# A gated mix of a long convolution and a token mixer on one core: first sine early, gate as array columns, four outputs finished in one step, two sets of transposes as transfers

## The chip, the cores and the metric

The kernel runs on one core of a Trainium2 chip. Its time is in device microseconds (us), from the start of the program to its end, as one launch. Five engines work side by side, each through its own list of instructions in order: TensorE (PE in the profile, with its weight loads as PEld), VectorE (DVE), ScalarE (ACT), GpSimd (POOL) and SyncE (SP), which here only issues transfers. An engine that waits for a semaphore holds up everything behind it in its own list.

## The reference

```python
def reference(A_q, A_k, A_v, A_shift_k, A_ssm_k, A_ssm_D, B_x, B_w1, B_w2, B_w3, B_w4, gate_w):
    x = A_q                                             # (1, 2048, 640), bf16
    g = sigmoid((x * gate_w).sum(-1, keepdims=True))
    # a: a causal convolution of 2048 taps for each of 640 channels, by FFT
    k_shift = sum over t < 4 of k_pad[:, t:t + S] * shift_k[:, 3 - t]
    kv = k_shift * v
    y = irfft(rfft(pad(kv)) * rfft(pad(ssm_k)))[:S] + kv * ssm_D
    a = x * y
    # b: layernorm, w1, gelu, a shift of the four channel quarters by +1, -1, +2, -2 tokens, w2
    h = gelu(layernorm(x) @ w1)                         # 640 -> 640
    x1 = x + shifted(h) @ w2                            # 640 -> 640
    b = x1 + gelu(layernorm(x1) @ w3) @ w4              # 640 -> 1536 -> 640
    return g * a + (1 - g) * b
```

## The kernel before

The 2048 tokens are held as 16 "slots" of 128 tokens (a token's partition comes from its high bits, its slot from the low four). The program is a list of some 770 small tasks. Each task names its engine, what it reads and writes, which buffers it takes and gives back. The order in which they are issued is written out by hand as a list of numbers (`ORDER`), the letter behind a number choosing the engine (a for ScalarE, v for VectorE, p for GpSimd). That one list fixes the order on each engine, and on SP that of the transfers. A small planner (`Plan.place`) walks through it only to choose buffers and the number of "fill" matmuls, which multiply zeros and keep TensorE's clock up where it expects a gap. PSUM has eight banks (pool `U`), taken singly or in pairs; transfers go out on eight semaphores in turn, so that the ninth one waits for the first to land.

The tasks that the change and the prediction name, with the lines of the profile:

| task | engine | what it does | line before |
|---|---|---|---|
| `fill` | PE | matmuls of zeros, 512 columns | 256 |
| `cjb.j`, `cj.j` | PE, ACT | row j of `shift_k` (transfer `ldCJ`) spread over all partitions, copied out of PSUM | 473, 387 |
| `phase`, `phsmall`, `phand`, `sin` | DVE, ACT | integer phases of the Fourier matrices from GpSimd's iotas, then one sine of 2272 columns into `TRIG` | 422 to 455, 459 |
| `st1.s`, `rs1.s`, `nm1.s` | DVE or ACT, POOL, DVE or ACT | mean and variance of slot s, its rstd, the normed rows | 521 to 542 |
| `tr1.s`, `ev1.s`, `evh.s` | PE, DVE or ACT | the normed rows of two slots transposed by TensorE, copied to `xnT`; halo slots | 548, 387/389 |
| `trh.c`, `evt.c` | PE, DVE or ACT | the filter `ssm_k` transposed | 762, 387/389 |
| `w1.G.p`, `g1`, `w2.s`, `x1.s`, `sq.s` | PE, ACT, PE, DVE, ACT | first MLP, gelu, second matrix, residual, sum of squares | 623/627, 640, 649, 656, 661 |
| `gate`, `gz`, `gtanh`, `gg` | PE, DVE, ACT, DVE | the gate's sums by token, and the two factors from them | 671/674, 681 to 684, 686, 691/692 |
| `kv3` ... `kv0` (`m`, `a`, `v`) | DVE | four taps, sums and the product with v, for four slots each | 782, 786, 790 |
| `s1h`, `s1x`, `e1h`, `e1x` | PE, ACT or DVE | first Fourier step of filter and of kv, copied to `FS` | 817/830, 387/389 |
| `wF`, `rF` | SP | `FS` written to DRAM, read back in another layout as `FX` | 842, 856 |
| `s2`, `e2`, `pa`/`pb`, `s3`, `e3` | PE, ACT/DVE, DVE, PE, ACT/DVE | second step, complex product, step back | 864, 387/389, 879, 892, 387/389 |
| `wG`, `rG`, `s4`, `yq` | SP, SP, PE, DVE | result through DRAM to `GX`, last step with matrix `BT`, times gate and q | 904, 924, 936, 942 |
| `bperm`, `trb`, `evb` | DVE, PE, DVE | the columns of `TRIG` put in order, 16 blocks transposed, copied to `BT` | 389, 917, 389 |
| `ve2`, `st2`, `nm2.s`, `dt2.s` | DVE, POOL, DVE or ACT, SP | second layernorm; a transfer that transposes a slot's normed rows | 700/701, 706 to 708, 540/542, 724 |
| `w3.c.f`, `g2.c.f`, `w4.s`, `t2.s` | PE, ACT, PE, DVE | third and fourth matrix for four slots (chunk c), residual | 732, 739, 746, 752 |
| `ad.s`, `st.s` | DVE, SP | the last mix, two slots stored together | 948, 382 |

The convolution and the MLP interleave. VectorE's `kv` work of the first half stands between the layernorms and the residuals; between the write of the last `wFx` and the first `s2` stand the four `w4` of chunk 0 on TensorE, and between the last `s3` and the first `s4` those of chunks 1 and 2.

Of the kernel before, what the change touches and what calls it, by code (L numbers as in the profile page):

```python
# [16 lines left out]
P = 128  # L17
# [19 lines left out]
0 60v 22 73a 1 74 7 2 21 20 23 71v 3 8 4 9 16 72 63a 5 64 61a 53v 70p 14 51v 62 12 54 79v 13a 75v 31 36 52 18 38  # L37
391 81v 6 66v 56v 24 17a 392v 32 82 89v 25 65a 15a 395 80 67 76v 30 34 90 396a 69v 387 388v 55v 77 37 83v 68a
393 47 35 57 78a 87a 84v 88 28 26 394v 389 97v 33 85 59a 86v 390v 92v 119 42 10 397 121 58a 98 27 95v 100v 113v
19 450 41 91a 93 94v 96 40 11a 99v 111v 39 400 120 451a 123 122 438 124 105v 439a 29 444 43 127 452 401 402 445a  # L40
440 441a 141 101 145 125 112 115v 398 128 102a 453a 142 146 44 149 150 442 446 106 126 443a 147 148 403 404 129
130 447a 454 405 143 114 138 139 455a 132 133 45 144 406 103a 154 155 456 458 399 157 116a 131 407 50 457a 104
107v 158 448 160 161 459a 411 449 108a 134 135 109 136 117 140 151 152 110a 118a 211 137 410 412 163 212 164 462
464 460 468 465a 463a 165 217 167 185 213v 469a 186 169 408 413 470 218 46 466 215v 409 168 221v 414 166 415 416
417 171 467a 471a 461 193 49 474 170 214 473 172 478 187 191 479a 176 177 421 472 194 475a 173 216 192 219a 480
174 220 188 420 482 189 481a 190 179 222 180 476 483a 477a 485 156 204 422 486 494 205 423 201 202 484 207 495a
490 492 424 48 208 487a 418 162 153 419 425 491a 488 489a 493a 223 496 198 224 498 199 497 500 501a 231 239 426
502 504 499a 506 232 243 503a 233 240 225 431 507a 182 427 430 432 505a 433 226 244 510 234 514 428 515a 509 183
# [12 lines left out]
691a 693 297 707 724 341 342 298 295 706 355 356 726 708 296 727 709 729 365 730 369 742 728 366 697 370 361 733
# [293 lines left out]
def build(env, nc, io):  # L355
# [36 lines left out]
    def c_iota(t):  # L392
# [3 lines left out]
        nc.gpsimd.iota(env.early("KC", [P, 64], I32)[:], pattern=[[4, 64]], base=1, channel_multiplier=0)  # L396
        nc.gpsimd.iota(env.early("PI", [P, 1], I32)[:], pattern=[[0, 1]], base=0, channel_multiplier=1)
# [3 lines left out]
    add("iota", "POOL", 2.2, c_iota, w=["iota"], roles=("C0",))  # L401

    def c_id(t):
        I = env["ID"]
        nc.gpsimd.memset(env["ONE"][:], 1.0)
        nc.gpsimd.memset(env.early("NPI", [P, 1], F32)[:], float(-np.pi * (1 - 2.0 ** -20)))
        nc.gpsimd.memset(I[:], 0.0)
        nc.gpsimd.affine_select(out=I[:], in_=I[:], compare_op=ALU.not_equal, fill=1.0, base=0, pattern=[[-1, P]],
                                channel_multiplier=1)
        nc.gpsimd.memset(env.sm("MH", [P, 2])[:], -0.5)  # L410
        nc.gpsimd.memset(env["K"][0:1, 0:3, :], 0.0)
    add("ident", "POOL", 2.9, c_id, w=["ID", "c0", ("K", "z")], roles=("C0", "K"))
# [27 lines left out]
    add("phsmall", "DVE", 2.6, c_small, r=["iota"], w=["ph0"], roles=("PRE", "C0"))  # L440
# [10 lines left out]
    for ri in range(2):  # L451
        add(f"phase{ri}", "DVE", 1.25, c_ph(ri), r=["iota"], w=[("ph", ri)], roles=("PRE", "C0"))
# [8 lines left out]
    add("sin", "ACT", 3.5, c_sin, r=["pha", "c0"], w=["TRIG"], roles=("PRE", "C0"))  # L461
# [94 lines left out]
    DMA1 = ()  # L556
# [108 lines left out]

    def gate(t):
        m = env.PS[:, t.buf["U"][0], :]
        gw = env.sm("GW", [P, 5], BF16)
        for s in range(16):
            for kb in range(5):  # L670
                nc.tensor.matmul(m[:, s:s + 1], lhsT=env["xnT"][:, s + 2, kb, :], rhs=gw[:, kb:kb + 1], start=(kb == 0),
                                 stop=(kb == 4))
        for kb in range(5):
            nc.tensor.matmul(m[:, 16:17], lhsT=env["ONE"][:], rhs=gw[:, kb:kb + 1], start=(kb == 0), stop=(kb == 4))
    tg = add("gate", "PE", 2.3, gate, r=["GW", "c0"] + [("xnT", s) for s in range(16)], acq=[ONE], mode="f", roles=("xnT",))

    def gz(t):
        m = env.PS[:, tg.buf["U"][0], :]
        z, sd = SS("Z"), SS("SD")
        sg = env.sm("SG", [P, 1])  # L680
        nc.vector.tensor_tensor(out=sd[:], in0=SS("VE")[:], in1=SS("RS")[:], op=ALU.mult)
        nc.vector.tensor_scalar(out=sg[:], in0=m[:, 16:17], scalar1=-1.0, scalar2=None, op0=ALU.mult)
        nc.vector.scalar_tensor_tensor(out=z[:], in0=SS("NB")[:], scalar=sg[:, 0:1], in1=m[:, 0:16], op0=ALU.mult, op1=ALU.add)
        nc.vector.tensor_tensor(out=z[:], in0=z[:], in1=sd[:], op=ALU.mult)
# [304 lines left out]
```

## Time and profile before

| | |
|---|---|
| time, median of 3 runs | 234.26 us (232.64 to 235.73) |
| the profiled execution | 233.85 us, of which 232.1 us are the span of its instructions |
| PE, DVE, ACT, POOL busy in the span | 95%, 81%, 67%, 17% |
| granted TensorE clock, mean | 0.988 |
| moved by transfers | 56.23 MB, 242 GB/s |

The span holds the core's instructions; 1.75 us of the execution lie outside it. A busy share is a mean over stages with different limits: what an edit is worth is read in its own stage, from the row of the wait that ends last there. In the chain of waits, each piece is what released the next, back from the last instruction. The busy time of a group of matmuls can be a little longer than the time that it takes from the chain, since matmuls overlap at their ends.

### The profile page before, as it was taken

Reading aid. Unit: us, or ns where it says so; the run is one execution under the profiler, and the core shown is the slowest. Engines: PE = TensorE matmul, PEld = TensorE weight load, DVE = VectorE, ACT = ScalarE, POOL = GpSimd, SP = SyncE. Lnnn points to the kernel's source line nnn. Section 1 sums busy time; section 2 is a strip of 40 time slices with the busy share of each in tenths; the row PEclk is TensorE's granted clock in tenths of the full one; section 3 lists DMA queues with packets and bytes.
Section 4 is the critical chain, followed back from the end, with each engine's and each line's share of the span. In section 5 each row is a group of like instructions: output and inputs, shape, how many; then the busy total and the mean of one; then the engine's idle time right before and its main releaser. Section 6 shows DMA issues by size and latency. Waiting matters only on the chain.

```text
span 232.1 us, 5340 instructions
## 1 busy us (share of the span) xinstructions
PE 220.8 (95%) x2143; PEld 108.6 (47%) x2163; DVE 186.9 (81%) x264; ACT 155.1 (67%) x221; POOL 40.5 (17%) x90
## 2 busy tenths in 40 slices
PE   7799999999999999999999999999999999999990
PEld 3158834456345744445543433344345554444550
DVE  5974699989999989997378998897986128887972
ACT  2996989988897998979669988888956004142000
POOL 7585317810700000011340000000000000000000
PEclk9979999999999999999999999999999999999998
DMA  5899889976999696867899995899843894968742
GB/s 149 280 277 303 198 237 272 330 270 206 289 294 283 196 266 224 270 224 250 191 315 300 327 349 177 255 228 310 204 172 135 242 406 147 282 187 248 233 109 57
DMA packets 39051, 56.23 MB, mean 242 GB/s; under 512 B 13809, under 2 KB 28914, under 8 KB 39026
## 3 DMA queue, kind: packets, MB, share of 16 engines
q1 hardware_dynamic: 39026, 55.88, 81.8%
q8 instruction: 17, 0.28, 0.5%
q14 instruction: 8, 0.07, 0.1%
HBM read 34.90 MB, written 18.35 MB: 229 GB/s over the span
## 4 chain that ended last, share of the span: by engine, by line
PE 80%; DVE 7%; DMA 4%; issue 2%; SPq 2%; ACT 2%; DVEq 0%; ACTq 0%
PE PS L746 21%; PE PS L732 18%; PE PS L649 8%; PE PS L623 7%; PE PS L864 4%; PE PS L892 4%; PE PS L762 3%; DMA FX<-FH 3%; PE PS L817 3%; DVE VC L786 3%; PE PS L256 2%; PE PS L936 2%; SPq L382 2%; PE PS L627 2%; DVE VC L782 2%
## 5 line engine op out<-in xcount | busy, mean ns | idle before, releaser
L746 PE MATMUL PS<-W,h2T 128*128 128x128 bf16 (+1 forms) x374 | 53.2, 297 | 0.5
L739 ACT ACTIVATE h2T<-PS 128x512 bf16<-128x512 f32 x48 | 28.1, 609 | 30.8 <-PE PS L732 30.0
L746 PEld LDWEIGHTS <-h2T 128*128 128x128 bf16 x384 | 29.6, 98 | 25.3 <-issue 2.5
L387 ACT CAST FS<-PS 128x1024 bf16<-128x1024 f32 x38 | 37.1, 1022 | 4.5 <-PE PS L817 2.6
L732 PEld LDWEIGHTS <-W 128*128 128x128 bf16 x240 | 21.2, 98 | 30.0 <-issue 8.5
L387 ACT CAST XH<-PS 128x1024 bf16<-128x1024 f32 x26 | 25.8, 1014 | 6.5 <-PE PS L864 6.4
L732 PE MATMUL PS<-x1nT,W 128*128 128x512 bf16 x120 | 28.8, 380 | 0.0
L732 PE MATMUL PS<-XB,W 128*128 128x512 bf16 x120 | 28.6, 380 | 0.0
L752 DVE TENSOR_TENSOR x<-PS,x 128x640 bf16<-128x640 f32 x16 | 13.1, 822 | 15.8 <-PE PS L746 15.8
L879 DVE TENSOR_TENSOR PP<-XH 128x2048 bf16<-128x2048 bf16 x20 | 23.6, 1219 | 0.9 <-PE PS L892 0.4
L782 DVE TENSOR_TENSOR VC<-K,VC 128x2560 bf16<-128x2560 bf16 x16 | 23.8, 1485 | 0.2
L649 PE MATMUL PS<-W,hsT 128*128 128x128 bf16 (+1 forms) x152 | 23.1, 295 | 0.4
L623 PE MATMUL PS<-xnT,W 128*128 128x512 bf16 x80 | 19.1, 380 | 0.5 <-ACT hsT L640 0.5
L389 DVE CAST XH<-PS 128x1024 bf16<-128x1024 f32 x14 | 16.7, 1219 | 2.8 <-PE PS L864 2.7
L649 PEld LDWEIGHTS <-hsT 128*128 128x128 bf16 x160 | 12.9, 98 | 11.5 <-issue 0.2
L786 DVE TENSOR_TENSOR VC<-VC 128x2560 bf16<-128x2560 bf16 x12 | 17.9, 1489 | 0.2
L942 DVE SCALAR_TENSOR_TENSOR W<-PS,GG,QO 128x640 bf16<-128x640 f32 x16 | 13.6, 879 | 4.4 <-PE PS L936 3.9
L706 POOL TENSOR_TENSOR r<-v,MH 128x2 f32<-128x2 f32 x8 | 6.9, 856 | 55.6 <-DVE v L701 55.5
L387 ACT CAST GS<-PS 128x1024 bf16<-128x1024 f32 x13 | 13.0, 1018 | 3.1 <-PE PS L892 3.1
L656 DVE SCALAR_TENSOR_TENSOR x<-PS,x 128x640 bf16<-128x640 f32 x16 | 13.1, 820 | 2.3 <-PE PS L649 2.0
L948 DVE SCALAR_TENSOR_TENSOR QO<-x,OG,W 128x640 bf16<-128x640 bf16 x16 | 13.6, 879 | 0.1
L864 PE MATMUL PS<-FX,TRIG 64*32 64x512 bf16 x320 | 12.9, 382 | 0.1
(106 smaller groups left out, 272.4 us busy)
## 6 DMA issues: line engine op xcount, KB each, us to landing
FH<-FS SPq DMA_DIRECT2D x8, 640.0 KB, 5.4
FXD<-FS SPq DMA_DIRECT2D x8, 640.0 KB, 4.6
FX<-FXD SPq DMA_DIRECT2D x10, 512.0 KB, 5.5
FX<-FH SPq DMA_DIRECT2D x10, 512.0 KB, 5.2
GX<-GD SPq DMA_DIRECT2D x8, 640.0 KB, 5.2
W<-in_B_w_dram SPq DMA_DIRECT2D x2, 1920.0 KB, 10.5
GD<-GS SPq DMA_DIRECT2D x8, 480.0 KB, 3.8
x<-in_A_q_dram SPq DMA_DIRECT2D x16, 160.0 KB, 4.9
```

Of the source, the lines that this page charges most:

```text
L387: nc.scalar.copy(out=out, in_=in_)
L389: (nc.vector if t.on == "DVE" else nc.gpsimd).tensor_copy(out=out, in_=in_)
L623: nc.tensor.matmul(m[:, b, :], lhsT=W[:, 0, kb, 160 * fb:160 * fb + 128], rhs=rhs(kb, shifts[fb]), start=(kb == 0), stop=(kb == 4))
L649: nc.tensor.matmul(m[:, c0:c1], lhsT=env["hsT"][:, o.buf["hs"][0], fb, 128 * (s % 4):128 * (s % 4) + 128], rhs=env["W12"][:, 1, fb, c0:c1] ...
L732: nc.tensor.matmul(env.PS[:, t.buf["U"][0], :], lhsT=env["W3"][:, kb, 128 * fb:128 * fb + 128], rhs=env.nT(int(nP[-1]))[:, :, kb, :], star ...
L739: nc.scalar.activation(out=env["h2T"][:, o.buf["h2"][0], fb, :], in_=env.PS[:, t.buf["U"][0], :], func=ACT.Gelu_apprx_tanh)
L746: nc.tensor.matmul(m[:, c0:c1], lhsT=env["h2T"][:, o.buf["h2"][0], fb, 128 * (s % 4):128 * (s % 4) + 128], rhs=env["W4"][:, fb, c0:c1], st ...
L782: nc.vector.tensor_tensor(out=VC[:, o], in0=env["K"][:, a + 3 - j:a + 7 - j, :], in1=w, op=ALU.mult)
L786: nc.vector.tensor_tensor(out=VC[:, 1], in0=VC[:, 1], in1=VC[:, 2], op=ALU.add)
L864: nc.tensor.matmul(env.U(t.buf["U"][0])[32 * j:32 * j + 32, gp, :], lhsT=CRI()[64 * gp:64 * gp + 64, 32 * pc:32 * pc + 32], rhs=X[64 * gp: ...
L879: nc.vector.tensor_tensor(out=env["PP"][:, o.buf["PP"][0], a, :].rearrange("p (b c) -> p b c", b=2), in0=X.unsqueeze(1).broadcast_to([P, 2 ...
L942: nc.vector.scalar_tensor_tensor(out=u, in0=env.Uf(t.buf["U"][0])[:, 0:D], scalar=SS("GG")[:, s:s + 1], in1=env["QO"][:, 2 * q.buf["Q"][0] ...
```

## The change

- A first sine of one element (`warm`) stands at the head of ScalarE's list, behind a two-element memset on VectorE. The iotas are split into those for `phase` and those for `phsmall`, and the constants into `ident`, `ones` and `kz`; `phase` now comes ahead of `phsmall`.
- The gate's weights are copied to 32 equal columns (`sg`), and the gate is 20 matmuls of 512 columns in four column groups in place of 85 of one column; VectorE transposes the result in blocks. A single matmul (`sgm`) gives the sum of the weights.
- For slots 12 to 15, `w4` is two tasks, of 512 and of 128 columns, in a bank each. `ax` first adds (1 - g) x1 to the convolution's part; `fo` then takes (1 - g) times the bank straight from PSUM and adds that. The slots are stored one by one.
- `bperm` goes to GpSimd, and `trb` with `evb` become one transposing transfer (`dbt`). The normed rows of slots 10 to 13 go through transposing transfers (`dt1`), as `dt2` does for the second layernorm, in place of `tr1.10`, `tr1.12`, `ev1.10` and `ev1.12`.
- The whole `ORDER` is another one (771 tasks). `ldCJ` is the fifth transfer and not the ninth; `ldw3` and `ldw4` change places on SP, with `ldw4` behind the writes of `s1x` group 8; 11 fills stand ahead of the first `cjb` and not 18.

```diff
+    add("warm0", "DVE", ..., c_warm, w=["WA"])        # memset of Z[:, 0:2]
+    add("warm", "ACT", ..., lambda t: nc.scalar.activation(out=Z[:, 1:2], in_=Z[:, 0:1], func=ACT.Sin), ...)
...
-    DMA1 = ()
+    DMA1 = (10, 12)
...
     def gate(t):
-        for s in range(16):
-            for kb in range(5):
-                nc.tensor.matmul(m[:, s:s + 1], lhsT=env["xnT"][:, s + 2, kb, :], rhs=gw[:, kb:kb + 1], ...)
         for kb in range(5):
-            nc.tensor.matmul(m[:, 16:17], lhsT=env["ONE"][:], rhs=gw[:, kb:kb + 1], ...)
+            for k in range(4):
+                nc.tensor.matmul(m[32 * k:32 * k + 32, :], lhsT=gb[:, kb, :], rhs=env["xnT"][:, 2:18, kb, 32 * k:32 * k + 32], ...)
...
     def gz(t):
+        for h in range(2):
+            nc.vector.transpose(out=T, in_=env.PS[:, tg.buf["U"][0], 256 * h:256 * h + 256])
+            nc.vector.tensor_tensor(out=z[:, c], in0=T.rearrange("p (s j) -> p s j", j=32)[:, :, 0], in1=z[:, c], op=ALU.subtract)
...
+            if s in LATE:                               # LATE = (12, 13, 14, 15)
+                for n, (c0, c1) in enumerate(((0, 512), (512, 640))):
+                    late[s, n] = add(f"w4.{s}.{n}", "PE", ..., w4n, acq=[ONE], **kw)
...
-    add("bperm", ...)                                   # in ORDER: on DVE
+    add("bperm", ...)                                   # in ORDER: on POOL
-    tb = add("trb", "PE", ..., trb, r=["BP", "ID"], acq=("U",), mode="f")
-    add("evb", ...)
+    dma("dbt", ..., lambda t: nc.sync.dma_start_transpose(out=env["BT"][:], in_=env.BP.rearrange("p s t -> p (s t)")), ...)
...
+                    u = env["W4"][:, 12 + y.buf["V"][0], :]                      # ax
+                    nc.vector.scalar_tensor_tensor(out=u, in0=x, scalar=OG[:, s:s + 1], in1=u, op0=ALU.mult, op1=ALU.add)
+                        nc.vector.scalar_tensor_tensor(out=QO[..., c0:c1],        # fo, n = 0 and 1
+                                in0=env.PS[:, bank, 0:c1 - c0], scalar=OG[:, s:s + 1], in1=u[:, c0:c1], op0=ALU.mult, op1=ALU.add)
```

The order of `s1x` group 0 and what surrounds it, on each engine, is in the changed list: TensorE `w2.12 w3.0.10 w3.0.2 w2.8 s1x.0 s1x.3 s1x.2 s1xr.0 w2.14 s1x.1 w4.3 w4.0 w4.1 w4.2 s2x.0.0 s2x.0.1 w3.1.0`; VectorE `kv0.v x1.12 x1.8 ve2.6 nm2.4 e1x.2 nm2.5 e1x.1 nm2.6 ve2.8 t2.3 x1.14 nm2.7`; SP `dt2.4 wFx.0.0 wFx.0.1 dt2.5 dt2.7 dt2.6 rFx.0 rFh.0`. Before it was TensorE `s1x.0 s1x.1 w3.0.6 s1x.3 s1xr.0 s1x.2 w4.1 w4.3 w4.2 w4.0 w3.1.0 s2x.0.0`; VectorE `kv0.v ve2.4 x1.12 e1x.0 nm2.4 e1x.2 bperm gg ve2.6 t2.1 nm2.5 nm2.7 nm2.6`.

Around the new `dt1` it is VectorE `kv3.m3 kv3.m2 kv3.a2 ev1.8 nm1.13 dfold x1.0 x1.3 nm1.12 kv3.m1 nm1.11 x1.1 nm1.10 x1.2 kv3.a1 kv3.m0 kv3.a0 kv3.v`, SP `wFh.4.0 ldk7 wFh.4.1 dt1.13 dt1.12 ldk9 dt1.10 dt1.11 ldw3 wFh.0.0`, and TensorE comes to `w1.2.0` behind six `w2` where there were eight. At the end it is TensorE `w4.14.0 w4.15.0 w4.14.1 s4.12 s4.13 w4.12.0 w4.12.1 w4.15.1 w4.13.0 w4.13.1`, VectorE `yq.11 yq.10 yq.4 ad.4 yq.5 ad.5 ad.10 ad.11 yq.15 yq.14 ax.14 ax.15 yq.12 ax.12 yq.13 fo.14.0 fo.14.1 fo.15.0 fo.15.1 fo.12.0 fo.12.1 ax.13 fo.13.0 fo.13.1`.

150 lines of the change are left out of this document (94 added, 56 removed), and 8 rows, old and new, of the table ORDER.

## The prediction

> **What bounds the kernel now.** I began with the page: the share of each engine, the slices, the chain that ended last.
>
> ```profile
> PE 220.8 (95%) x2143; PEld 108.6 (47%) x2163; DVE 186.9 (81%) x264; ACT 155.1 (67%) x221; POOL 40.5 (17%) x90
> PE   7799999999999999999999999999999999999990
> DVE  5974699989999989997378998897986128887972
> PE 80%; DVE 7%; DMA 4%; issue 2%; SPq 2%; ACT 2%; DVEq 0%; ACTq 0%
> ```
>
> TensorE is full from the third slice to the last but one, and 80% of the chain is its own. So the time is TensorE's work, plus a start, plus a tail. But 7% of the chain is VectorE's, and the slices show where: it too is full from the seventh slice to the seventeenth. The stage view (length, then PE, PEld, DVE, ACT and POOL busy, clock, share of the transfer engines) sizes this.
>
> ```profile
> 0.00:29.00 29.00, 25.75 (x244) 15.93 (x247) 19.96 (x51) 21.45 (x30) 17.37 (x51) 0.94 0.87 241
> 29.00:60.00 31.00, 30.32 (x244) 14.77 (x246) 29.09 (x49) 28.04 (x42) 12.34 (x16) 1.00 0.88 262
> 60.00:101.10 41.10, 40.80 (x363) 20.00 (x365) 39.61 (x47) 36.40 (x53) 4.10 (x6) 1.00 0.88 251
> 117.00:154.00 37.00, 37.00 (x489) 14.26 (x495) 33.01 (x33) 31.18 (x41) 1.50 (x5) 1.00 0.95 272
> ```
>
> From 29 to 101.1 VectorE is busy 68.7 of 72.1 us and TensorE 71.1: two engines with the same end. Where they meet is in the timeline:
>
> ```profile
> 99.62 1.49 DVE L790 TENSOR_TENSOR K<-VC 128x2560 bf16<-128x2560 bf16 x1
> 101.17 0.61 PE L817 MATMUL PS<-K,TRIG 64*128 64x512 bf16 x4
> 103.65 13.21 PE L746 MATMUL PS<-W,h2T 128*128 128x512 bf16 x94
> 103.76 1.22 DVE L389 CAST FS<-PS 128x1024 bf16<-128x1024 f32 x1
> 105.44 1.27 SPq L842 DMA_DIRECT2D FXD<-FS  x2
> 112.80 0.46 SPq L856 DMA_DIRECT2D FX<-FXD  x1
> 116.70 1.24 PE L732 MATMUL PS<-XB,W 128*128 128x512 bf16 x5
> 117.87 0.63 PE L864 MATMUL PS<-FX,TRIG 64*32 64x512 bf16 x16
> ```
>
> VectorE's last product `kv0.v` ends at 101.1 and `s1x` of group 0 starts at once. Its results go out at 105.4, come back from 112.8 on, and `s2` starts at 117.87; the four `w4` (13.2 us) and one `w3` fill TensorE meanwhile. I call this the joint. Work taken off TensorE ahead of it counts only as far as VectorE comes earlier too.
>
> **The change part by part: the front.** The start:
>
> ```profile
> 0.72 5.06 SPq L382 DMA_DIRECT2D x<-in_A_q_dram  x8
> 8.66 0.72 PE L473 MATMUL PS<-C,ONE 1*128 1x512 bf16 x2 [1.74 <-DMA C<-in_A_shift_k_dram]
> 13.94 1.99 PE L762 MATMUL PS<-ID,SK 128*64 128x128 bf16 x32
> 28.58 1.24 PE L623 MATMUL PS<-xnT,W 128*128 128x512 bf16 x5
> 20.60 0.45 DVE L542 TENSOR_SCALAR xn<-x,RS,NB 128x640 bf16<-128x640 bf16 x1 [2.24 <-PE PS L548]
> L527 ACT ACT_TABLE_LOAD x1 | 1.3, 1283 | 4.6 <-DMA x<-in_A_q_dram 4.6
> ```
>
> Eight issues take 5.06, 0.63 each. `ldCJ` fifth and not ninth is four issues earlier: `cjb` at 6.1 instead of 8.66. All four `cjb` with their fills come first (pairs at 1.2 us, plus six fills), and the first `trh` follows at about 13.0, against 13.94; the first filter block is issued no earlier than before (behind nine loads and two small ones), so little more can come of it. Five `trh` of 1.9, four `tr1` and 11 fills later, `w1.0.0` is at about 28.2, with the fourth `cjb` and one `s1h` already done, which before came behind it: 1.4 us for TensorE. Two table loads instead of three take 1.28 from ScalarE while it waits for x anyway.
>
> VectorE does `phase` and `phsmall` while x is on its way. By the end of the fourth `evt` (26.4, against 26.6) it has one `st1`, one `evt` and two `ev1` more behind it, and one `evh` and two `nm1` fewer: 2.1 us ahead. Up to `kv0.v` its whole list costs the same: two `x1` fewer (1.7), one `evh` fewer (1.1), one `ev1` and one `nm1` more (1.25), `sg` 0.35, and `gz`. The last two have no row. `gz` was four small operations, 0.7; its two block transposes read 256 columns of PSUM each: at least 0.15 (a small operation), at most the 1.22 of the 1024-column copy above; by columns 0.35, so 0.85 more in all. Sum: about zero. Later waits stay alike (at `x1.0` it waits some 1.5 us for the early `w2`), so I take 2.5 us at `kv0.v`: 98.6. Without that lead 0; with the `gz` bound -1.7.
>
> TensorE's own gains ahead of it:
>
> ```profile
> 34.95 1.19 PE PS L627 x20
> 55.17 1.12 PE PS L548 x20
> 79.13 1.98 PE PS L671 x80
> 129.06 1.00 PE PS L917 x16
> ```
>
> The 20 gate matmuls are of the form of 34.95, four column groups of 512: 1.2 plus 0.1 for `sgm` against 1.98 and five more, 0.8 saved. `tr1.10` and `tr1.12` save 1.12. With the start, TensorE comes to `s1x.0` at about 98, VectorE at 98.6: these 1.9 us are hidden by VectorE.
>
> And the joint is longer now. `w4.3` takes the pair of banks of `s1x.2`, whose copy stands behind `x1.12`, `x1.8`, `ve2.6` and `nm2.4` on VectorE:
>
> ```profile
> L656 DVE SCALAR_TENSOR_TENSOR x<-PS,x 128x640 bf16<-128x640 f32 x16 | 13.1, 820 | 2.3 <-PE PS L649 2.0
> FX<-FXD SPq DMA_DIRECT2D x10, 512.0 KB, 5.5
> x1nT<-xn SPq DMA_TRANSPOSE x8, 6.1
> W<-in_B_w_dram SPq DMA_DIRECT2D x2, 1920.0 KB, 10.5
> ```
>
> That is 0.82 + 0.82 + 0.3 + 0.44 + 1.22 and the gaps, 3.8 after `kv0.v`, where 101.1 to 103.65 was 2.55. `w4` starts at 102.4 (before 103.65) and ends at 115.6; `s2x.0.0` follows without the `w3` between. The read-back stands on SP behind `dt2.7` and `dt2.6`, hence behind `t2.3` (102.4 + 3.3 + 0.8), `x1.14` (0.9) and `nm2.7`: 107.9, two issues of 1.25, `rFx.0` at 110.5, landed 5.1 to 5.5 later, 115.8. Before, `s2` began at 117.87 with a `w3` of 1.08 done: equal to 116.8. So 1.0 us of the front arrives behind the joint, 2.5 at best, 0 at worst.
>
> `ldw4` now follows `wFx.8`, so four issues behind the end of `kv1.v`; it has 17.6 us from there (13.7 of VectorE's list, then 3.9) and needs about 4.3 to be issued and 10.5 to land: 2.8 to spare.
>
> **Middle.** `trb` is 1.00 less on a TensorE that is busy 37.00 of 37.00. VectorE (89%) and ScalarE (84%) follow closely and its `evb` goes too: I take 0.9, between 0 and 1.0. `dbt` moves 3.2 times the data of a `dt2`: between 6.1 and 20 us to land, an issue of 1.25 to 4, with three later loads behind it; `s4` is over 20 us away, which hides it. `bperm` on GpSimd:
>
> ```profile
> L389 DVE COPY XB<-TRIG 128x2048 bf16<-128x2048 bf16 x1 | 1.3, 1311 | 0.0
> L411 POOL MEMSET K<- 1x1920 bf16 x1 | 1.7, 1688 | 0.0
> L408 POOL TENSOR_SCALAR_AFFINE_SELECT ID<-ID 128x128 bf16<-128x128 bf16 x1 | 0.4, 351 | 0.1
> ```
>
> By the memset's columns 1.8, by those of the select 5.6; I take 4. Behind it is `st2.8`, whose rows are wanted only for the third chunk, 20 us on: nothing.
>
> **Tail.**
>
> ```profile
> 222.80 3.43 PE L746 MATMUL PS<-W,h2T 128*128 128x512 bf16 x24
> 226.27 0.82 DVE L752 TENSOR_TENSOR x<-PS,x 128x640 bf16<-128x640 f32 x1 [0.30 <-PE PS L746]
> 227.13 0.89 DVE L948 SCALAR_TENSOR_TENSOR QO<-x,OG,W 128x640 bf16<-128x640 bf16 x1
> ```
>
> TensorE ends at 226.23, VectorE 1.8 later. Now only `fo.13.1` must follow, 128 columns, 0.16 by columns of the 0.82 row and 0.3 with a start: 0.4 behind TensorE at best. But VectorE has, from `yq.5` on, twelve operations of about 0.84 and four `fo` pairs of about 0.95 (one more start than the 0.82 row), 13.9 us, beginning about 1.7 behind `s4.5`, while TensorE needs 14.4 from there: VectorE would end 1.2 behind. So 0.6 to 1.4 less; the last store is half as large; I take 1.0.
>
> Sum against the profiled execution, 233.85: 1.0 + 0.9 + 1.0 = 2.9, 230.9. Its median is 0.2% above, so I say 231.0.
>
> **The rivals.** *TensorE stays the only bound.* For it: all slices of 9; against it: 99.62 and 101.17. Then the hidden 1.9 count, the 1.4 of the start, 1.0 and 1.4 of the tail: 5.7 less, 228.2.
>
> *The front brings nothing* (the early sine and `ldCJ` shorten only waits that VectorE's list does not have). For it: the slack was ScalarE's, and VectorE's early waits end on TensorE and loads. Then 1.9 remain: 232.0; with the `gz` bound 233.7.
>
> *GpSimd's copy holds VectorE.* `bperm` starts when `w2.14` is done, just where VectorE's `nm2.6` and `nm2.7` open the way for `rFx.0`. If the two exclude each other, `nm2.7` is up to 3.8 later and TensorE waits as long: 231.9 to 234.7. Rows for it: none; POOL's small operations ran beside VectorE's. The Trainium skill's page "SBUF — State Buffer", section "SBUF: two separate sides", states such a rule: VectorE in its two-port modes and a GpSimd operation hold a shared pair of ports for the whole instruction, and the other waits; by it the sum would be this rival's, for the copy from SBUF that moves here. No run yet shows it.
>
> *The new transfers are late: slower.* `dt1.10` stands behind `nm1.10` on VectorE, and `w1.2.0` needs its slot. Before:
>
> ```profile
> 53.50 0.44 DVE L542 TENSOR_SCALAR xn<-x,RS,NB 128x640 bf16<-128x640 bf16 x1
> 57.65 1.08 PE PS L623 x5
> ```
>
> `nm1.10` came at 53.50, behind four more `kv3` steps of 1.49; now I have it at 46, landed at 52.1, and `w1.2.0` at 53 (two `w2` and 1.12 fewer ahead of it). But its statistics are ScalarE's, behind seven gelus and copies. If `nm1.10` comes as late as before, the transfer lands at 60, TensorE idles 7 us, and `ldw3`, `wFh.0` and `ldv2` wait behind it on SP: 238. It decides from 51 on, where the gain is eaten.
>
> **How the numbers follow.** My sum (229.6 to 232) 0.42; TensorE alone 0.22; nothing in front 0.14; the port 0.08; late transfers 0.14. Range 227.0 to 237.0: below it a tenth, above it the worse half of the late transfers. 2% is about what a measurement of this kernel can tell: under 229.6 lie the second case and a third of the first, 0.36; over 238.9 part of the last and what I overlook, 0.10; the rest 0.54.
>
> **What would show it.** Right: first `cjb` near 6.1; `kv0.v` ending near 98.6 with TensorE waiting for it; `s2x.0.0` near 116; 0.3 to 0.5 us per `gz` transpose; last VectorE operation about 1 us behind TensorE. Wrong: TensorE idle ahead of `w1.2`, in the `w4` of chunk 0 (W4 not landed), or several us ahead of `s2x.0.0`; VectorE operations stretched beside `bperm`.

## The result and the profile after

The changed kernel takes 231.07 us (median of 4 runs, 230.72 to 232.48), the kernel before, on the same chip, 235.00 (232.64 to 236.47): a ratio of 0.9892, 95% interval 0.9844 to 0.9941. Ratios here are of fast runs alone, without those over 1.5% above the fastest of their kernel (such as the 236.47), and are not the quotients of the medians beside them. A second set gave 230.70 against 233.55, a ratio of 0.9892 (0.9858 to 0.9926). So it is 1.1% faster: inside the 2% to which the prediction gave 0.54, and at its 231.0. The profiled execution took 230.98 us, its span is 229.2; the difference of the spans, 2.9 us, is the number that the sum of the prediction gave. Its terms are not the predicted ones, as the rest shows.

The page after, shares, slices and the chain that ended last:

```profile
PE 219.9 (96%) x2058; PEld 103.5 (45%) x2058; DVE 189.9 (83%) x271; ACT 151.8 (66%) x220; POOL 45.1 (20%) x91
PE   7999999999979999989999999999999999999992
DVE  7984998998999999997469999889876328877992
PE 65%; DVE 11%; SPq 6%; DMA 5%; ACT 5%; issue 4%; POOL 2%; DVEq 0%; ACTq 0%
```

TensorE's share of the chain fell from 80% to 65%, VectorE's rose from 7% to 11%, and the row of TensorE has a 7 in its twelfth slice (63 to 69 us), where there was a 9. The view by stage says the same, cut at the end of `kv0.v` (99.04), at `s2x.0.0` (116.31), at the end of the last `s3` (176.50) and at TensorE's end (225.06); the columns are length, then PE, PEld, DVE, ACT and POOL busy, clock, share of the transfer engines and GB/s:

```profile
0.00:29.00 29.00, 26.95 (x252) 16.00 (x253) 23.34 (x58) 21.62 (x31) 16.15 (x50) 1.00 0.84 238
60.00:99.04 39.04, 37.33 (x259) 16.08 (x257) 38.33 (x43) 32.89 (x48) 5.04 (x5) 1.00 0.89 264
99.04:116.31 17.27, 16.33 (x122) 8.77 (x123) 11.36 (x29) 11.13 (x22) 8.15 (x15) 1.00 0.86 240
116.31:176.50 60.19, 59.92 (x833) 23.63 (x834) 52.39 (x48) 49.38 (x62) 0.23 (x2) 1.00 0.96 271
176.50:225.06 48.56, 48.56 (x340) 24.41 (x340) 35.65 (x46) 7.84 (x13) 0.00 (x0) 1.00 0.69 223
225.06:229.20 4.14, 0.00 (x0) 0.00 (x0) 0.39 (x2) 0.00 (x0) 0.00 (x0) 1.00 0.27 65
```

From 60 us to `kv0.v` VectorE is busy 38.33 of 39.04 us, TensorE only 37.33: before, TensorE had 40.80 of 41.10 there. The first row has a clock of 1.00 where the kernel before had 0.94; that part of the gain differs from run to run (see the last section). The same two stages of the kernel before, cut at the same events:

```profile
117.87:178.06 60.19, 59.37 (x842) 24.54 (x844) 52.54 (x50) 49.54 (x62) 0.74 (x3) 1.00 0.85 244
178.06:226.23 48.17, 47.91 (x343) 24.68 (x340) 32.86 (x40) 8.06 (x13) 0.00 (x0) 1.00 0.75 237
```

The middle is as long as before and holds one `w3` (1.08) more, the one that stood ahead of `s2x.0.0`: 1.1 us gained. The last stage is 0.39 longer. The rest: `s2x.0.0` came at 117.87 and now at 116.31, 1.56 earlier, less that `w3`: 0.5. From TensorE's end to the span's end it was 232.10 - 226.23 = 5.87 and is 4.14: 1.7. The sum is 0.5 + 1.1 - 0.4 + 1.7 = 2.9.

The timeline around the joint, after, the rows that answer to those of `kv0.v`, `s1x`, `w4` and the read-back before:

```profile
97.55 1.49 DVE L824 TENSOR_TENSOR K<-VC 128x2560 bf16<-128x2560 bf16 x1
99.09 1.13 PE L851 MATMUL PS<-K,TRIG 64*128 64x512 bf16 x6 [0.25 <-DVE K L824]
100.58 0.40 PE L864 MATMUL PS<-K,TRIG 64*128 64x128 bf16 x8 [0.35 <-DVE x L670]
102.69 13.21 PE L771 MATMUL PS<-W,h2T 128*128 128x512 bf16 x96
102.59 2.49 POOL L389 COPY XB<-TRIG 128x2048 bf16<-128x2048 bf16 x1 [0.30 <-PE PS L663]
104.01 1.25 DVE L556 TENSOR_SCALAR xn<-x,r,SB 128x640 bf16<-128x640 bf16 x1
106.17 0.82 DVE L786 TENSOR_TENSOR x<-PS,x 128x640 bf16<-128x640 f32 x1 [0.58 <-PE PS L771]
112.39 0.45 SPq L890 DMA_DIRECT2D FX<-FXD  x1
116.31 0.62 PE L898 MATMUL PS<-FX,TRIG 64*32 64x512 bf16 x16 [0.40 <-DMA FX<-FXD]
```

TensorE comes to `s1x.0` ahead of `kv0.v` and waits 0.25 for it, as predicted; `w4` starts 3.65 behind `kv0.v` (predicted 3.8). `nm2.6` (104.01) takes 1.25 in place of 0.44, for as long as GpSimd's copy `bperm` lasts: what the port rival said. But the next thing that VectorE needs comes later still, it waits 0.58 for TensorE at `t2.3`.

The same happens once more, at a place that the prediction did not look at. This is the timeline after, from 59 to 68 us:

```profile
59.97 1.69 POOL L418 MEMSET K<- 1x1920 bf16 x1
60.06 1.78 DVE L556 TENSOR_SCALAR xn<-x,r,SB 128x640 bf16<-128x640 bf16 x1 [0.45 <-POOL SB L732]
66.20 0.82 DVE L670 SCALAR_TENSOR_TENSOR x<-PS,x 128x640 bf16<-128x640 f32 x1
67.08 0.39 PE L851 MATMUL PS<-HT,TRIG 64*128 64x512 bf16 x2 [1.39 <-DVE x L670]
```

In splitting the constants the change made a task of its own, `kz`, of GpSimd's memset of K, and its list put it at 59.97. The `nm2` beside it (the long row of VectorE) takes 1.78 instead of 0.44: it ends 0.18 behind the memset's end, 1.34 late. Here VectorE has no pause to make up for it: the `x1` at 66.20 is late, and TensorE waits 1.39 for it. That is the 7 in the slices.

**The theory to test**, then: VectorE sets the front from 57 us to `kv0.v`, so the memset costs what it holds and the new gate costs what it adds to VectorE; TensorE sets the middle, VectorE the tail. Against it: that the long `nm2` is an accident and TensorE sets all. A useful measure, since the first 30 us vary from run to run, is the stretch from the first `w1` to the end of `kv0.v`: 28.58 to 101.11 = 72.53 before, 27.09 to 99.04 = 71.95 after, and 71.93 in the second trace of the same kernel (`again`, below). It is called the stretch from here on. Behind it, from the end of `kv0.v` to TensorE's end, the traces of the versions whose middle and tail are as changed have 125.3 to 126.1, so a difference of the stretch arrives at the end only to within 0.8.

### The profile page after: what moved, and what is told of

Same layout as the page of the kernel before. It is cut to its first block, busy times and chain, and to the rows that moved or that the text cites. A ratio compares the mean times of both kernels' runs of the same rounds, so it can differ in the third digit from the quotient of the medians.

```text
span 229.2 us, 5179 instructions
## 1 busy us (share of the span) xinstructions
PE 219.9 (96%) x2058; PEld 103.5 (45%) x2058; DVE 189.9 (83%) x271; ACT 151.8 (66%) x220; POOL 45.1 (20%) x91
## 4 chain that ended last, share of the span: by engine, by line
PE 65%; DVE 11%; SPq 6%; DMA 5%; ACT 5%; issue 4%; POOL 2%; DVEq 0%; ACTq 0%
PE PS L757 24%; PE PS L771 13%; PE PS L663 6%; PE PS L778 5%; PE PS L898 5%; PE PS L926 4%; DMA x<-in_A_q_dram 3%; DMA FX<-FH 2%; PE PS L964 2%; SPq L382 2%; DVE x L670 2%; PE PS L637 2%; DVE VC L820 2%; DVE VC L816 2%; PE PS L851 2%
## 5 line engine op out<-in xcount | busy, mean ns | idle before, releaser
L764 ACT ACTIVATE h2T<-PS 128x512 bf16<-128x512 f32 x48 | 28.2, 604 | 31.4 <-PE PS L757 29.5
L387 ACT CAST FS<-PS 128x1024 bf16<-128x1024 f32 x38 | 37.6, 1019 | 4.5 <-PE PS L851 3.2
L771 PE MATMUL PS<-W,h2T 128*128 128x512 bf16 (+1 forms) x288 | 40.1, 299 | 0.1
L757 PEld LDWEIGHTS <-W 128*128 128x128 bf16 x240 | 20.7, 98 | 30.8 <-issue 10.6
L771 PEld LDWEIGHTS <-h2T 128*128 128x128 bf16 x288 | 22.2, 98 | 19.0 <-issue 1.9
L387 ACT CAST XH<-PS 128x1024 bf16<-128x1024 f32 x22 | 21.8, 1014 | 5.4 <-PE PS L898 5.4
L389 DVE CAST XH<-PS 128x1024 bf16<-128x1024 f32 x18 | 21.9, 1222 | 3.0 <-PE PS L898 1.8
L663 PE MATMUL PS<-W,hsT 128*128 128x512 bf16 (+1 forms) x160 | 23.8, 299 | 0.0
L786 DVE TENSOR_TENSOR x<-PS,x 128x640 bf16<-128x640 f32 x12 | 9.9, 824 | 15.5 <-PE PS L771 15.4
L730 POOL TENSOR_TENSOR r<-v,MH 128x2 f32<-128x2 f32 x8 | 8.3, 1042 | 53.8 <-DVE v L725 53.8
L387 ACT CAST GS<-PS 128x1024 bf16<-128x1024 f32 x15 | 14.7, 1017 | 5.0 <-PE PS L926 5.0
L778 PE MATMUL PS<-W,h2T 128*128 128x512 bf16 (+1 forms) x96 | 13.4, 299 | 0.0
```

The source lines that it names most:

```text
L387: nc.scalar.copy(out=out, in_=in_)
L389: (nc.vector if t.on == "DVE" else nc.gpsimd).tensor_copy(out=out, in_=in_)
L663: nc.tensor.matmul(m[:, c0:c1], lhsT=env["hsT"][:, o.buf["hs"][0], fb, 128 * (s % 4):128 * (s % 4) + 128], rhs=env["W12"][:, 1, fb, c0:c1] ...
L757: nc.tensor.matmul(env.PS[:, t.buf["U"][0], :], lhsT=env["W3"][:, kb, 128 * fb:128 * fb + 128], rhs=env.nT(int(nP[-1]))[:, :, kb, :], star ...
L764: nc.scalar.activation(out=env["h2T"][:, o.buf["h2"][0], fb, :], in_=env.PS[:, t.buf["U"][0], :], func=ACT.Gelu_apprx_tanh)
L771: nc.tensor.matmul(m[:, c0:c1], lhsT=env["h2T"][:, o.buf["h2"][0], fb, 128 * (s % 4):128 * (s % 4) + 128], rhs=env["W4"][:, fb, c0:c1], st ...
```

## The experiments

**The memset of K early.** On GpSimd, in the names of the order:

```diff
-iotb ident ones rs1.0 ... st2.0 st2.2 kz st2.4
+iotb ident ones kz rs1.0 ... st2.0 st2.2 st2.4
```

> The changed kernel with one instruction moved: GpSimd's memset of K (1x1920, 1.69 us, at 59.97 in the changed kernel) goes back to the first microseconds, right behind `ones`. In the changed kernel VectorE's `nm2` beside that memset took 1.78 us (60.06) where such an operation takes 0.44, and 4 us later TensorE waits 1.4 us for an `x1`. Theory (the two exclude each other, and VectorE is co-critical there): the `nm2` at about 60 takes 0.44 again, the 1.4 us wait for `x1` mostly goes, `kv0.v` ends at 97.7 to 98.5 (was 99.04), and the time is 0.5 to 1.2 us less than the changed kernel's 231.07, so 229.9 to 230.6. Rival 1 (the stretch is of something else, or VectorE has slack there): `nm2` stays long, or gets short and the time stays at 231.1 within 0.3. At its new place the memset may hold an operation of VectorE's `phand` by up to 0.4, hidden by the wait for x.

229.68 us, ratio 0.9817 (0.9774 to 0.9860). The stretch is 28.02 to 98.62 = 70.60, so 1.34 less than the 71.94 of the changed kernel's two traces: the time for which `nm2` was held. Its timeline has

```profile
60.97 0.45 DVE L557 TENSOR_SCALAR xn<-x,r,SB 128x640 bf16<-128x640 bf16 x1 [0.45 <-POOL SB L733]
66.22 0.83 PE L852 MATMUL PS<-HT,TRIG 64*128 64x512 bf16 x4
```

and no wait at that matmul. The time is 1.0 below the 230.70 of the second set and 1.4 below the 231.07 of the first, although this profiled execution ran its first 30 us at a clock of 0.94; the rival falls. Behind `kv0.v` it is 125.33 to TensorE's end, against 126.02 in the changed kernel: another 0.7, of which 0.5 lies ahead of `s2x.0.0`, where TensorE no longer waits for the read-back. Why the read-back comes earlier there stays open.

**The mirror: the kernel before with its memset late.**

```diff
-        nc.gpsimd.memset(env["K"][0:1, 0:3, :], 0.0)        # in "ident", at 3 us
+    add("kz", "POOL", 1.7, ...)                             # behind st2.2
```

> The mirror: the kernel before, with GpSimd's memset of K (1x1920, 1.69 us) moved from the first microseconds to a place behind `st2.2`, where VectorE works on `kv`, `x1` and `nm2` without a pause. If the memset excludes VectorE's one-input operations: one `nm2` takes 1.2 to 1.8 instead of 0.44, the stretch from the first `w1` to the end of `kv0.v` grows from 72.5 to 73.5 to 73.9, and the time grows by 0.8 to 1.4 us over the kernel before's. Rival (the long `nm2` was an accident of that place): no change in either, within 0.3.

235.16 us, against 233.55 for the kernel before in the same set; ratio 1.0081 (1.0052 to 1.0110).

```profile
63.56 2.34 DVE L542 TENSOR_SCALAR xn<-x,r,nb 128x640 bf16<-128x640 bf16 x2
64.03 1.69 POOL L412 MEMSET K<- 1x1920 bf16 x1
```

Two `nm2` take 2.34 in place of 0.9, and they end at 65.90, again 0.18 behind the memset. The stretch grows by 0.73 (28.18 to 101.44 = 73.26), less than the 1.0 to 1.4 that I expected: the hold itself is 1.4, half of which this order had to spare. The time grows by 1.6, more than the 0.8 to 1.4 expected, and what of it lies outside the stretch stays open; all six runs of this kernel had a mean clock of 0.990 or less, which the last section comes to. In both directions one instruction of GpSimd, on one partition, moves the whole kernel by 0.8%, by these ratios.

**`bperm` on VectorE.**

```diff
-POOL: st2.6 bperm st2.8
+DVE:  x1.14 nm2.7 bperm ve2.10
```

> The changed kernel with `bperm` (the 128x2048 copy) back on VectorE, behind `nm2.7`, where it takes 1.3. If GpSimd's copy holds VectorE: `nm2.6` at about 104 takes 0.44 again instead of 1.25. Theory (the hold is hidden, since VectorE then waits 0.58 for TensorE at `t2.3`): the time stays within 0.3 of 231.07. Rival (the hold costs at the joint): the read-back of FX lands earlier, the 0.40 wait ahead of `s2x.0.0` goes, and the time is 0.4 to 0.8 less.

232.07 us, ratio 0.9898 (0.9847 to 0.9950), so no better by the ratio, and 1.0 more by the time, outside the 0.3 of the theory. In the profiled execution the loss lies ahead of the joint: the first `w1` comes at 28.90, 1.8 later than in the changed kernel, after a loss of clock (last section), and from there to the end of `kv0.v` it is the same 71.94. `nm2.6` is short again, and it bought nothing: from the end of `kv0.v` to `s2x.0.0` it is 17.38, with 0.51 of wait there (17.27 and 0.40 in the changed kernel).

```profile
105.82 0.44 DVE L557 TENSOR_SCALAR xn<-x,r,SB 128x640 bf16<-128x640 bf16 x1
```

The same mechanism costs 1.34 at one place and nothing at the other. What decides is whether VectorE waits for something else next.

**The old front whole, then its halves.** First the old gate and the TensorE transposes together:

```diff
-    DMA1 = (10, 12)
+    DMA1 = ()            # PE: s1h.2 tr1.12 tr1.10 w2.4; ACT: g1.1.2 ev1.12 ev1.10
-gate: 20 matmuls of 512 columns, sgm, gz with two block transposes
+gate: 85 matmuls of one column, gz without
```

> The changed kernel with the old gate (a matmul for each slot, the rows of four small operations) and with `tr1.10` and `tr1.12` on TensorE: 1.9 us more of TensorE ahead of `s1x`, and 1.4 less of VectorE, by the durations of their rows. Theory (VectorE sets the end of the front, TensorE's 1.9 are hidden): from the first `w1` to the end of `kv0.v` 70.5 to 72.0 where the changed kernel has 71.9, the time 230 to 231.3. Rival (TensorE sets it): 72.5 to 73.8 for that stretch, and a time of 231.8 to 233.

237.22 us, ratio 1.0133 (1.0090 to 1.0175), outside both expectations. It does not decide between them, because my place for the transposes brought something of its own. TensorE's timeline, then the view by stage:

```profile
52.18 0.72 PE L563 MATMUL PS<-ID,xn 128*128 128x128 bf16 x10 [1.31 <-ACT xnT L388]
54.21 4.05 PE L664 MATMUL PS<-W,hsT 128*128 128x512 bf16 x15 [1.31 <-ACT xnT L388]
```

```profile
54.00:57.00 3.00, 2.79 (x11) 1.37 (x11) 0.00 (x0) 3.00 (x6) 0.00 (x0) 0.50 0.00 0
71.00:75.00 4.00, 4.00 (x20) 1.88 (x18) 3.93 (x8) 2.31 (x5) 0.00 (x0) 0.59 1.35 223
```

Two waits of 1.31, and behind them 3 us at half clock; then 4 us at 0.59 behind the one-column matmuls of the gate. Waits 2.6, clock 3.0 x 0.50 + 4.0 x 0.41 = 3.1: together 5.7, and the stretch is 77.63, 5.7 more than 71.94. That leaves nothing for the 1.9 of matmuls themselves, and the run says nothing about them. So the halves were run by themselves.

The gate alone, with its 85 one-column matmuls at the place of the new ones:

> The changed kernel with the old gate alone, at the place of the new one: 80 matmuls of one column and five more (2.2 us) instead of 20 of 512 columns (1.25), and the rows by four small operations of VectorE instead of two block transposes and five small ones (0.9 to 1.2 less). Theory (VectorE sets the end of the front): the stretch from the first `w1` to the end of `kv0.v` stays at 71.9 or falls by up to 1.0; the time 229.8 to 231. Rival 1 (TensorE sets it): +1.0 in both, 231.7. Rival 2 (the clock): in an earlier run with the old gate the granted clock fell to a half for 3 us, 2 to 3 us behind these one-column matmuls; if that is their doing and not a chance of that run, the mean clock of most runs is below 0.995 and the time 1.2 to 2.5 longer.

230.55 us, ratio 0.9854 (0.9808 to 0.9901). The stretch is 27.85 to 98.93 = 71.08, 0.87 *less*: the new gate, which saves TensorE 0.9 (2.2 for 1.25), makes the front of this kernel longer by what it adds to VectorE. TensorE's 0.9 more goes into the pause that the memset's hold makes just behind it: the wait of 1.39 is 0.48 here. Its two block transposes,

```profile
L705 DVE STREAM_TRANSPOSE W<-PS 128x256 f32<-128x256 f32 x2 | 0.9, 445 | 0.0
```

are most of that. The clock did not fall behind the one-column matmuls here, so that it did so in the run above was not their doing alone.

The transposes alone:

```diff
-SP: dt1.13 dt1.12 ldk9 dt1.10 dt1.11
+PE: s1h.2 w2.4 tr1.10 tr1.12 w2.7 w1.2.0;  ACT: e1h.3 ev1.10 ev1.12
```

> The changed kernel with the rows of slots 10 to 13 transposed by TensorE again (`tr1.10`, `tr1.12`, 1.12 us, and two copies of 1.23 on ScalarE) right behind `w2.4`, and no `dt1`. Theory (TensorE had that much to spare ahead of `kv0.v`): the stretch from the first `w1` to the end of `kv0.v` grows by 0 to 0.4, the time stays within 0.4 of 230.7. Rival 1 (TensorE bound): +1.1. Rival 2 (ScalarE's copies make `w1.2` wait, as they made TensorE wait 1.3 us twice in the run with the whole old front): +1.5 to 3, with a wait for `xnT` in the trace and a lower clock behind it.

233.03 us, ratio 0.9972 (0.9939 to 1.0005): nearly all of the change's gain is gone. The stretch is 27.86 to 101.71 = 73.85, 1.9 more. The theory falls: TensorE had next to nothing to spare at 50 us. The two rivals are both in it, the transposes themselves and a wait for ScalarE's copies; the lower clock of the second did not come. VectorE's timeline of this run,

```profile
54.20 0.82 DVE L671 SCALAR_TENSOR_TENSOR x<-PS,x 128x640 bf16<-128x640 f32 x1 [1.83 <-PE PS L664]
```

has VectorE waiting 1.83 for the `w2` that stands behind the transposes (1.28, and 0.76 of waiting for `xnT`): 2.04 of delay became 1.83 of waiting, so TensorE had 0.2 to spare. The transposes alone would cost some 1.1 there (an estimate, 1.28 less 0.2); the rest is a wait that this undo brought with it. So the front has two parts. In the changed kernel VectorE waits for TensorE three times up to 44 us (1.2 in all), and at 51 us the two are still within 0.2 of each other; from 57 us on it never waits for TensorE, and TensorE waits for it.

**The start as before.** No early sine, CJ as the ninth load:

```diff
-SP: ldx0 ldx14 ldCJ ldx2 ldx4          ACT: warm sin ...
+SP: ldx0 ldx14 ldx2 ldx4 ... ldCJ      ACT: sin ...
```

> The changed kernel without the early sine and with CJ as the ninth load and not the fifth; the rest of the order stays. The first `cjb` comes at 8 to 8.7 instead of 5.7 to 6.0. Theory (the start is a delay for all that follows): the first `w1` 0.8 to 1.5 later than with the new start at the same clock, the time 231.6 to 232.6. Rival (the start only shortens waits that come anyway, for x and the filter's first block): the first `w1` within 0.4 and the time within 0.4 of the changed kernel's.

231.81 us, ratio 0.9940 (0.9910 to 0.9969), 1.1 more than `again` in its set, so the time is as the theory has it. The trace does not settle how: the first `cjb` is at 8.39 and the first `w1` at 27.72, against 26.91 and 27.09 in the two traces of the changed kernel, all at full clock in the first 30 us; but other kernels here with the new start and a full clock have it anywhere from 26.96 (`best`) to 28.11 (`tail_back`), with waits for transfers between. From the first `w1` to the end of the span it is 201.9 against 202.1, so what the start is worth lies ahead of it. A part is likely the clock (last section).

**`trb` on TensorE again.**

```diff
-SP: dbt
+PE: s2x.2.1 trb s2h.4.1;  DVE: evb behind e2h.4.0
```

> The changed kernel with the last matrix B transposed again by TensorE (`trb`, 1.0 us, with VectorE's `evb`), behind `s2x.2.1`, and no `dbt`. Theory (TensorE bounds the middle, 59.9 busy of 60.2 us): 0.8 to 1.1 us slower than 231.07, so 231.9 to 232.2, all of it between `s2x.0.0` and the last `s3`. Rival (VectorE or ScalarE bound the middle, and TensorE's time is hidden): within 0.3 of 231.07.

233.14 us, ratio 0.9975 (0.9942 to 1.0009). From `s2x.0.0` to TensorE's end it is 116.73 to 227.27 = 110.54, 1.79 more than 108.75:

```profile
130.02 1.07 PE L951 MATMUL PS<-ID,XB 128*128 128x128 bf16 x16
132.47 1.24 PE L758 MATMUL PS<-XB,W 128*128 128x512 bf16 x5 [0.83 <-DVE BT L390]
```

1.0 of transposes, and 0.83 for a bank that `evb` frees late at this place; the kernel before had no such wait behind its `trb`. Both come out at TensorE's end (1.79 of 1.83), so TensorE sets the middle. The time is 2.1 above 231.07, twice what the theory had (0.8 to 1.1): the wait was not in it.

**The old tail.**

```diff
-    LATE = (12, 13, 14, 15)     # w4 in two banks, ax and fo, single stores
+    LATE = ()                   # w4 whole, t2 and ad, stores in pairs
```

> The changed kernel with the old end alone: `w4.12` to `w4.15` whole, followed by `t2` and `ad`, and the last outputs stored in pairs as before. Theory (the end is VectorE's: it ended 0.4 behind TensorE's last matmul instead of 1.8, and the span ended 3.75 behind VectorE instead of 4.08): 1.4 + 0.3 more, less 0.4 of TensorE that the finer groups cost: 1.0 to 1.7 us slower than 231.07, so 232.1 to 232.8, and VectorE's last operation again 1.7 to 1.9 behind TensorE's. Rival (the last store sets the end whatever comes ahead): 0.3 slower at most.

233.11 us, ratio 0.9971 (0.9932 to 1.0009). The ends of the two, the changed kernel first:

```profile
217.70 7.36 PE L778 MATMUL PS<-W,h2T 128*128 128x512 bf16 x60
224.43 1.02 DVE L984 SCALAR_TENSOR_TENSOR QO<-PS,OG,W 128x512 bf16<-128x512 f32 x2 [0.53 <-PE PS L778]
```

```profile
219.34 6.69 PE L771 MATMUL PS<-W,h2T 128*128 128x512 bf16 x48
226.07 0.82 DVE L786 TENSOR_TENSOR x<-PS,x 128x640 bf16<-128x640 f32 x1 [1.52 <-PE PS L771]
226.94 0.89 DVE L996 SCALAR_TENSOR_TENSOR QO<-x,OG,W 128x640 bf16<-128x640 bf16 x1
```

VectorE ends at 225.45, 0.39 behind TensorE, against 227.83, 1.80 behind. From `s2x.0.0` to the span's end it is 114.32 against 112.89: 1.4, of which VectorE 1.41, the store 0.22 (3.97 against 3.75), and TensorE -0.20.

**The changed kernel again**, as a control of the second set:

> The changed kernel itself, beside the others of this set. From the first result: 231.07 within 0.6. From the first `w1` to the end of `kv0.v` 71.9 us (71.95 in its first trace), the `nm2` at about 60 held to 1.78 again; the first `w1` itself moves with the clock of the first 30 us (27.1 to 28.9 in the four traces with this start so far).

230.70 us (229.97 to 232.63); the stretch is 26.91 to 98.84 = 71.93.

**The joint.** With the memset early, two more edits:

```diff
-DVE: t2.3 x1.14 nm2.7            PE: w4.2 s2x.0.0 s2x.0.1 w3.1.0
+DVE: t2.3 nm2.7 x1.14            PE: w4.2 w3.1.0 s2x.0.0 s2x.0.1
```

> A candidate for a faster version: the changed kernel with the memset of K early (229.68 alone), `x1.14` behind `nm2.7` on VectorE (0.9 ahead of what opens the read-back of FX), and one `w3` moved ahead of `s2x.0.0` on TensorE. Theory (what is left at the joint is the way from `kv0.v` to the read-back): TensorE no longer waits ahead of `s2x.0.0`, and the stretch from the end of `kv0.v` to the end of TensorE, 125.3 us with the memset early, falls by 0.3 to 0.9: 228.8 to 229.4. Rival (TensorE has no pause left there worth the name, since it waited only 0.35 to 0.56 us): within 0.2 of 229.68.

229.76 us, ratio 0.9837 (0.9790 to 0.9884): no better than the memset alone (229.68), as the rival had it. There was nothing left to gain: with the memset early TensorE already did not wait ahead of `s2x.0.0`. Now another wait stands behind it, in the waits of TensorE:

```profile
PE PS L899 <- DVE XH L390: 0.6, 1, 0.6
```

`s2` comes earlier and finds VectorE's copy of the bank not done. From the end of `kv0.v` to TensorE's end it is 126.08, against 125.33.

**What the runs point to**: the memset early and the old gate, all else as changed.

> A version made of what the runs showed: the changed kernel with the memset of K early and the old gate, both of which took time off VectorE's list between 57 us and `kv0.v` (1.34 and 0.86 of the stretch from the first `w1` to the end of `kv0.v`, 71.94 in the changed kernel). Theory (VectorE alone sets that part, so the two add): the stretch is 69.6 to 69.9, and the time 228.9 to 229.4. Rival (with VectorE 1.3 earlier the one-column gate matmuls, 0.9 more of TensorE, come onto the path): the stretch is 70.3 to 70.8, and the time 229.5 to 229.9, as with the memset alone.

229.39 us, ratio 0.9802 (0.9746 to 0.9858), the lowest of all, though not resolved from the memset alone. The stretch is 26.96 to 97.38 = 70.42: the rival's number, only 0.18 gained. The time lies in the theory's range, but not for its reason: from the first `w1` to the end of the span it is 200.3, against 200.1 with the memset alone, and the first `w1` came earlier (26.96 against 28.02). In the view by stage

```profile
60.00:97.38 37.38, 37.38 (x319) 17.39 (x318) 36.06 (x40) 32.24 (x47) 3.38 (x3) 1.00 1.00 273
```

TensorE is full again, and VectorE is busy 36.06 of the 37.38. Without the memset's hold TensorE has no pause behind the gate, so it no longer matters much which of the two carries it.

## Why the prediction was right, and where only its sum was

The direction and the rough size came out because the picture of the joint, the middle and the tail held. That the sum came out to 0.1 is luck: the front gave 0.5 less than forecast, the middle 0.2 and the tail 0.35 more, and the clock, which the prediction did not count, differs between the two traces.

**The front (predicted 1.0, measured 0.5).** The picture was right: `kv0.v` sets the end, `w4` starts 3.65 behind it, TensorE waits for VectorE at `s1x.0`. Two terms were missed, of opposite sign.
- "Up to `kv0.v` its whole list costs the same" left out `kz`. The order showed it on GpSimd behind `st2.2`; I put the port rival at `bperm` alone and gave it 0.08. From the predicted first `w1` (28.2) to the predicted `kv0.v` (98.6) are 70.4 us; with the memset early it is 70.60. So the list was summed nearly rightly, and the hold of 1.34 is most of the error of 1.55.
- The first `cjb` came at 5.67 (predicted 6.1) and the first `w1` at 27.09, not 28.2. My durations of the start came from an execution with a clock of 0.94 in the first 29 us, a row that I quoted and did not use. By stage, the kernel before and the changed one:

```profile
6.00:9.00 3.00, 1.26 (x6) 0.38 (x4) 2.96 (x3) 2.90 (x7) 1.16 (x2) 1.00 0.80 213
11.00:15.00 4.00, 4.00 (x28) 1.75 (x27) 3.11 (x10) 3.47 (x5) 3.23 (x11) 0.57 1.08 263
```

```profile
6.00:9.00 3.00, 3.00 (x12) 0.62 (x11) 2.90 (x7) 2.25 (x3) 1.65 (x4) 1.00 0.85 177
11.00:15.00 4.00, 3.75 (x49) 2.95 (x50) 3.90 (x11) 3.18 (x8) 3.29 (x9) 1.00 0.92 303
```

  Before, TensorE waits for CJ from 6.9 to 8.7, and from 11 to 15 us its clock is 0.57, worth 1.7 of matmuls (4 x 0.43). The changed start has no such gap and, in this trace, no such loss.

**"These 1.9 us are hidden by VectorE"** is the step that failed outright. The gate's 0.8 were hidden, in the pause that the memset made, and the gate itself cost 0.87 on VectorE, whose price (0.85) I had right; with the memset early it costs 0.18. The transposes' 1.12 were not hidden: undoing them costs 1.9 of the stretch, some 1.1 of it theirs, because at 51 us VectorE is only 0.2 behind TensorE. I had read the front as one stage with one bound; 68.7 and 71.1 busy of 72.1 us, on the two engines, allow both readings.

**The middle (0.9, measured 1.1)**: the mechanism held, and `trb_back` shows the size of `trb`, 1.07. That the whole came so near is in part chance: by the rows by stage TensorE's idle time there fell from 0.82 to 0.27 and its other work grew by some 0.5 (59.37 less 1.0, against 59.92 less 1.08). `dbt` was issued in 6.18 us, above my bound of 4, and landed in 8.3; both stayed hidden, as `s4` was far.

**The tail (1.0, measured 1.35 = 1.41 + 0.33 - 0.39).** The failed step is "VectorE would end 1.2 behind": it ended 0.39 behind, the "0.4 at best" of the sentence before, and had 0.53 to wait for the last bank. That TensorE's last stage would be longer, by 0.39 against the kernel before and by 0.20 against the old tail, had no term at all; the likely cause, not tested by itself, is eight groups of `s4` and `w4` in place of six.

**The rivals.** *TensorE alone* (228.2) is false after 57 us, and at 51 us it holds to within 0.2. *The front brings nothing* is false by the 0.5, though the spread from trace to trace of the first `w1` is as large. *Late transfers* is false:

```profile
44.80 2.55 SPq L586 DMA_TRANSPOSE xnT<-xn  x2
51.13 1.24 PE L637 MATMUL PS<-xnT,W 128*128 128x512 bf16 x5
```

`dt1.10` and `dt1.11` are issued at 44.80 (I had 46) and `w1.2.0` starts without a wait. *The port* is true as a mechanism, at another place than I priced. "Rows for it: none" was a misreading: GpSimd's timeline of the kernel before has

```profile
58.95 1.88 POOL L706 TENSOR_TENSOR r<-v,MH 128x2 f32<-128x2 f32 x1 [8.94 <-DVE v L701]
101.46 0.71 POOL L706 TENSOR_TENSOR r<-v,MH 128x2 f32<-128x2 f32 x1 [36.98 <-DVE v L701]
```

The first starts 0.17 behind a two-input product of VectorE (58.78 to 60.27) and takes 1.2 longer than the same operation does elsewhere.

## What to carry to other kernels

- Where two engines are both above 95% in a stage, look for the hand-over inside it: which of the two waits for the other early, and which late. An edit that moves work from one to the other gains on one side of that point and loses on the other; here the gate cost 0.87 behind it, and the transposes gained some 1.1 ahead of it.
- Cost every instruction that changes its place, also the ones that no sentence of the change speaks of: the dearest here was a memset of one partition. What holds another engine is free only where that engine waits anyway.
- Read the clock's column before taking durations from a stretch, and undo one part at a time: an undo of two parts brought waits and clock losses of its own, three times the size of what it was to measure.

## What the runs showed of the hardware that I had not expected

- **GpSimd and VectorE hold each other.** Three times (memset at 59.97 after, memset at 64.03 in the mirror, copy at 102.59 after) a one-input operation of VectorE from SBUF to SBUF ended 0.18 us behind the end of GpSimd's instruction, 0.8 to 1.4 late; VectorE's copy out of PSUM beside `bperm` (1.23) was not held. The other way round, GpSimd's power in `st2` takes 1.89 the two times that it starts beside a two-input product of `kv`, and 0.71 to 0.87 the six other times (its timeline, after):

```profile
57.55 1.89 POOL L730 TENSOR_TENSOR r<-v,MH 128x2 f32<-128x2 f32 x1 [0.90 <-DVE v L725]
...
108.51 0.71 POOL L730 TENSOR_TENSOR r<-v,MH 128x2 f32<-128x2 f32 x1 [1.52 <-DVE v L725]
```

  The Trainium skill, page "SBUF — State Buffer", section "SBUF: two separate sides", says that the two share a pair of ports as an exclusive lock: whichever starts first, a GpSimd operation or a VectorE operation in a two-port mode (or with two SBUF inputs, against a GpSimd operation that reads SBUF), has it for the whole instruction. These rows agree in both directions.
- **A loss of clock lasted 3.4 us or twice that, and a pause of TensorE alone does not decide it.** By the clock of single microseconds, TensorE was at half clock for 3.4 us from 11.4 in the kernel before, whose wait of 1.74 had ended at 8.66. In the old front it was so for 3.4 us from 53.8, at the end of two waits of 1.31 with 0.7 of matmuls between, and for 3.4 us again from 70.9, with no pause since 57. `bperm` on VectorE, with the new start, lost 6.8 us from 9.5, though TensorE had not paused since 2.46; it has

```profile
11.00:15.00 4.00, 4.00 (x38) 2.37 (x38) 3.30 (x11) 3.10 (x7) 3.20 (x10) 0.50 1.01 328
```

  and its first `w1` at 28.90. The Trainium skill, page "TensorE: Matmul & The Clock Gate", section "Part 1: The HAM clock gate (the "warmup" mystery)", ties the half clock to an idle window of some 3.4 us, and says that the windows run freely. The length of the losses and the chance agree; that an idle window stands ahead of each does not, since the pauses here are shorter and two losses had none. The old start with a wait of 1.08 lost nothing in its profiled execution.

  Over the runs that the ratios count, the mean clock was under 0.994 in 40 of 62 of the kernel before (median 234.1 us, against 232.9 in the other 22), in 2 of 10 of the changed kernel, and in 8 of 12 of the changed kernel with the old start. At 0.994 and above the two kernels differ by 232.9 - 230.7 = 2.2; the medians of the second set differ by 2.8, so some 0.6 of the gain is the clock's (an estimate). That the earlier CJ keeps it up is likely from these counts, but no run varied the wait for CJ alone.
- **A transposing transfer's issue grows with its size** (SP's timeline, after):

```profile
102.47 1.25 SPq L749 DMA_TRANSPOSE XB<-xn  x1
...
160.22 6.18 SPq L947 DMA_TRANSPOSE BT<-XB  x1
```

  The first is 128x640, the second 128x2048: 3.2 times the data, 4.9 times the issue.
